# Hash-masked attention and a two-layer block on one core: score products in bursts of three key tiles, one hash for q and k, another order

## The chip, the core and the metric

The kernel runs on one core of a Trainium2 chip. The core has five engines that work side by side, each through its own queue in order: TensorE (PE, matrix products; its weight loads are shown as PEld), VectorE (DVE), ScalarE (ACT), GpSimd (POOL) and SyncE (SP, which here only issues DMAs). An engine waits for another one by semaphores. Matrix products are written to PSUM, which has eight banks of 512 fp32 values on each of 128 partitions; all else lies in SBUF. The metric is the device time of one execution in microseconds (us); lower is better.

## The reference, cut to what matters

```python
# q, k, v: 4 batches, 8 heads, 768 rows, 64 columns; proj: 64 x 6
q_bits = (einsum('bhsd,dk->bhsk', q, proj) > 0)      # six bits for each row
k_bits = (einsum('bhsd,dk->bhsk', k, proj) > 0)
mask   = q_bucket[:, :, :, None] == k_bucket[:, :, None, :]
scores = where(mask, (q @ k.T) / 8, -1e9)
attn   = exp(scores - max);  attn = attn / (sum(attn) + 1e-9)
x      = (attn @ v) with the heads side by side      # 4 x 768 x 512
xn     = (x - mean) / sqrt(var + 1e-6) * g_ln
out    = x + relu(xn @ w_ch1) @ w_ch2                # 512 -> 2048 -> 512
```

A query attends only to the keys with the same six bits.

## The kernel before, in words

The rows are cut into 12 units of 256 query rows, three to each batch of 768 rows. Within a unit the eight heads form two groups of four.

**Scores.** A step `S.s` is one unit, one head group and one pair of key tiles (128 keys each), so there are 72 steps. For each key tile and each of the four heads three products accumulate: one over the hash bits (line 569, tile `G`; 6 rows, 32 in the first batch) and two over the halves of the 64 columns (32 rows each, tiles `qb`, `kb`). The four heads sit in four groups of 32 rows of TensorE, each writing its own bank, so that four products run beside each other. Equal bits give a term so large that the exponential of all others vanishes. A step fills two tiles of two banks each (`sc`, tag `pp`, three such slots, six banks). ACT takes the exponential of each with `E.s.h` (line 575) into `E`, and `A.s` (line 594) multiplies it with the values and a column of ones into `acc`, which takes one of the same three slots. The other two banks (tag `f`) serve everything else on TensorE.

**From attention to output.** On DVE `na` and `nb` divide by the row sums, `nc` and `ag` take mean and variance, `ce` normalises into `xc`; `fl` transposes it by DMA into `xnT` (in unit 0 TensorE does this with `ft`, and `fc` on DVE scales by `g_ln`). `F.u.p` (line 658) is a piece of the first layer, 256 of the 2048 hidden columns: it reads columns 256 p to 256 p + 255 of `w1_sb`. `R` applies the relu on ACT or DVE. The second layer is `D` and `Z` in unit 0; the later units use seven half-sized products `P` with sums `ss` and `Y` (lines 725 and 730). `O` writes the output.

**Hash.** For batch 0 the row-wise q and k are transposed in 128 x 256 pieces (`tn`), hashed (`ha`, `hc`, `sl`, lines 393, 404, 417) and cast (`ca`). For later batches `LX` loads one head group of q or k (786 KB) with SP, `tu` transposes it on DVE into `T` (two slots, one tile for q and one for k), `CA` casts it, and `hm` (line 525) hashes it, 16 fp32 products of 192 columns, q's and k's apart. `bt` takes the signs, `mw` and `mr` spread the bits through DRAM into `G`.

**Weights.** `lw1.n` and `lw2.n` load a quarter of each weight matrix, with a cast from fp32 to bf16, from POOL's queue (lines 445 and 456): `lw1.n` brings columns 512 n to 512 n + 511 of `w1_sb`, `lw2.n` the rows 512 n to 512 n + 511 of the second matrix. `wg` later multiplies `g_ln` into `w1_sb`, `sw` makes the sums of weights that `P` uses.

**Order.** Nothing plans at run time. The string `ORDER` lists every operation as name, engine letter (t TensorE, v DVE, a ACT, p POOL, s SP) and indices; each engine's queue has its own words in that order. `SLOTS` gives, for each tag, the slot that each tile takes in turn. Semaphores between engines follow from the tiles that operations share. A DMA waits in its issuing engine's queue, and all behind it wait too.

Of the kernel before, what the change touches and what calls it, by code (L numbers as in the profile page):

```python
# [10 lines left out]
AOP = mybir.AluOpType  # L11
# [5 lines left out]
lp.a lx.a.0.1.0.1 lx.s.0.0.0.1 lx.s.0.1.1.3 lx.s.1.1.0.3 lx.s.1.0.0.1 lv.s.0.0.4 lx.s.0.0.1.3 lv.s.0.4.4 lx.s.1.0.1.3  # L17
lg.s on.p.0 mem.v tab.a pf.v warm.t wm.t.0 wm.t.1 sel.p tn.v.0.0.0
p32.p tn.v.0.1.0 on.p.1 ca.a.0.0.0 pmem.p ha.t.0.0.0 bh.v.0.0.0 ha.t.0.1.0 bh.v.0.1.0 wm.t.2
wm.t.3 ca.a.0.1.0 tn.v.0.1.1 ca.p.0.1.1 tn.v.0.1.2 S.t.0.2 E.a.0.0 E.a.0.1 ha.t.0.1.1 bh.v.0.1.1  # L20
ha.t.0.1.2 bh.v.0.1.2 wm.t.6 tn.v.1.1.1 ca.p.1.1.1 lw1.p.3 ca.a.0.1.2 tn.v.1.1.0 S.t.1.2 E.a.1.1
tn.v.1.0.0 ha.t.1.1.1 bh.v.1.1.1 cv.p.0.0.0 tn.v.1.1.2 gx.p.1.0.0 S.t.2.2 cv.p.0.0.2 cv.p.0.4.2 ca.p.1.1.2
E.a.1.0 ca.a.1.0.0 lv.s.1.0.3 lw1.p.1 ha.t.1.0.0 bh.v.1.0.0 gx.p.1.0.1 LX.s.1.0.0 ha.t.1.1.2 bh.v.1.1.2
E.a.2.1 lw1.p.0 ca.v.1.1.0 LX.s.1.0.1 tn.v.0.0.1 S.t.4.2 E.a.2.0 lv.s.1.0.2 ca.v.0.0.1 E.a.4.1
ha.t.1.1.0 A.t.0.2 A.t.2.2 sq.t.0.0 E.a.4.0 bh.v.1.1.0 S.t.3.2 sc.v.0.0 A.t.1.2 cv.a.0.4.0
E.a.3.1 hc.t.0.0.1 E.a.3.0 lw2.p.0 na.v.0.0 S.t.5.2 bc.v.0.0.1 sl.t.0.0.1 bi.v.0.0.1 E.a.5.1
sq.t.0.4 tn.v.1.0.1 S.t.8.2 hc.t.1.0.1 nb.v.0.0 nc.v.0.0 E.a.5.0 bc.v.1.0.1 E.a.8.0 A.t.4.2
A.t.5.2 sc.v.0.4 A.t.3.2 na.v.0.1 nb.v.0.1 E.a.8.1 sl.t.1.0.1 ca.a.1.0.1 bi.a.1.0.1 S.t.6.2
gt.t E.a.6.0 nc.v.0.1 ag.v.0.1 S.t.7.2 ag.v.0.0 ce.v.0.1 ft.t.0.1 ce.v.0.0 gc.v
E.a.6.1 E.a.7.0 ft.t.0.0 S.t.9.2 E.a.7.1 E.a.9.0 fc.v.0.1 E.a.9.1 fc.v.0.0 F.t.0.3  # L30
A.t.7.2 R.a.0.3 F.t.0.7 R.a.0.7 S.t.10.2 tn.v.1.0.2 E.a.10.0 tu.v.1.0.1.2 gx.p.1.1.0 LX.s.1.1.0
lw1.p.2 tu.v.1.0.1.3 tu.v.1.0.0.3 lv.s.1.0.1 E.a.10.1 tn.v.0.0.2 hc.t.0.0.2 ca.a.0.0.2 tu.v.1.0.1.0 A.t.6.2
bc.v.0.0.2 sl.t.0.0.2 F.t.0.6 R.a.0.6 lw2.p.3 A.t.8.2 bi.v.0.0.2 S.t.11.2 F.t.0.0 tu.v.1.0.0.1
hc.t.1.0.2 tu.v.1.0.1.1 gx.p.1.1.1 LX.s.1.1.1 na.v.1.0 tu.v.1.0.0.0 lw2.p.1 E.a.11.0 rs.p.0 tu.v.1.0.0.2
R.v.0.0 E.a.11.1 CA.v.1.0.0 S.t.14.2 E.a.14.0 nb.v.1.0 bc.v.1.0.2 E.a.14.1 hm.t.1.0 ca.v.1.0.2
lv.s.1.0.0 S.t.12.2 wg.v.3 sl.t.1.0.2 bi.a.1.0.2 bt.v.1.0 mw.s.1.0 mr.s.1.0.1 A.t.11.2 A.t.10.2
tu.v.1.1.0.3 E.a.12.1 A.t.9.2 CA.p.1.0.1 na.v.1.1 nb.v.1.1 mr.s.1.0.2 mr.s.1.0.0 tu.v.1.1.0.1 tu.v.1.1.0.2
E.a.12.0 nc.v.1.0 F.t.0.2 R.a.0.2 S.t.13.2 E.a.13.1 su.p.1.0 F.t.0.4 F.t.0.5 R.v.0.5
S.t.16.2 lw2.p.2 E.a.13.0 A.t.12.2 E.a.16.0 A.t.13.2 A.t.14.2 tu.v.1.1.0.0 F.t.0.1 E.a.16.1
tu.v.1.1.1.1 tu.v.1.1.1.3 R.a.0.4 na.v.2.0 tu.v.1.1.1.2 tu.v.1.1.1.0 nc.v.1.1 nb.v.2.0 R.a.0.1 S.t.15.2  # L40
E.a.15.0 nc.v.2.0 mr.s.1.0.3 ag.v.1.0 E.a.15.1 hm.t.1.1 S.t.17.2 D.t.0.0.0 sw.v.3.1 E.a.17.0
ag.v.1.1 rs.p.1 bt.v.1.1 D.t.0.0.1 wg.v.1 lv.s.1.4.3 A.t.16.2 A.t.15.2 E.a.17.1 A.t.17.2
na.v.2.1 nb.v.2.1 mw.s.1.1 S.t.18.2 ce.v.1.1 LX.s.2.0.0 mr.s.1.1.3 fl.s.1.1 mr.s.1.1.1 nc.v.2.1
sw.v.2.1 ce.v.1.0 fl.s.1.0 cv.p.1.0.0 wg.v.2 wg.a.0 D.t.0.1.0 ag.v.2.0 sw.v.4.1 ag.v.2.1
mr.s.1.1.0 E.a.18.1 mr.s.1.1.2 D.t.0.1.1 sw.v.1.1 D.t.0.0.2 cv.a.1.0.2 CA.a.1.1.0 S.t.20.2 E.a.20.1
lv.s.1.4.2 E.a.20.0 D.t.0.0.3 Z.v.0.0 D.t.0.1.2 D.t.0.1.3 Z.v.0.1 S.t.19.2 F.t.1.6 E.a.18.0
rs.p.2 F.t.1.3 CA.p.1.1.1 E.a.19.0 S.t.21.2 O.s.0.0 lv.s.1.4.1 E.a.19.1 A.t.19.2 E.a.21.0
R.v.1.6 sw.v.3.0 sw.v.2.0 E.a.21.1 F.t.1.0 R.a.1.0 lv.s.2.0.3 R.v.1.3 ce.v.2.1 sw.v.4.0
lv.s.1.4.0 ce.v.2.0 F.t.1.5 A.t.20.2 S.t.22.2 fl.s.2.1 tu.v.2.0.0.2 F.t.1.4 R.a.1.5 cv.p.1.4.0
A.t.18.2 E.a.22.0 R.v.1.4 F.t.1.2 sp.t.1.0 sc.v.1.0 na.v.3.0 E.a.22.1 S.t.23.2 F.t.1.7  # L50
R.a.1.2 R.v.1.7 E.a.23.1 cv.v.1.4.2 E.a.23.0 F.t.1.1 sw.v.1.0 fl.s.2.0 LX.s.2.0.1 R.a.1.1
nb.v.3.0 S.t.24.2 E.a.24.0 E.a.24.1 on.p.2 P.t.1.2 Y.v.1.2 F.t.2.1 R.a.2.1 su.p.1.4
# [36 lines left out]
nc.v.6.1 F.t.5.5 tu.v.3.1.1.1 ag.v.6.0 S.t.48.2 E.a.48.0 ag.v.6.1 E.a.48.1 tu.v.3.1.1.2 tu.v.3.1.0.2
F.t.5.1 R.v.5.1 A.t.46.2 rs.p.6 R.a.5.5 ce.v.6.1 fl.s.6.1 A.t.45.2 A.t.47.2 na.v.7.1  # L90
# [698 lines left out]
```

## Time and profile before

| | before |
|---|---|
| three runs | 291.16, 291.59 and 295.0 us, median 291.59 |
| profiled execution, first to last instruction (span) | 289.9 us; the page gives no other time for it |
| PE busy | 283.2 us (98%) |
| DVE, ACT, POOL busy | 207.5, 206.2, 53.5 us |
| exponentials on ACT (line 575) | 144, 153.1 us |
| first-layer products (line 658) | 768, 94.2 us |
| score products (line 569) | 1728 |
| granted TensorE clock | 0.997 |
| DMA moved | 34.10 MB |

A row of a group of instructions gives line, engine, operation, output and inputs, shapes and count; then busy time and the mean length of one in ns; then the idle time of the engine before them and what ended it. Busy time of PE contains the modelled ends of pipelined products, which overlap. The page's slices cut the span into 40 parts of 7.2 us; a digit of 9 is 90% or more. In a table by windows the columns are the stretch, its length, busy time and count of PE, PEld, DVE, ACT and POOL, the granted clock, the share of the 16 DMA engines that was busy (it may pass 1.00, since packets overlap) and GB/s. Queue q1 is that of the DMAs that SP issues, q0 that of POOL's loads. The row of a DMA issue ends with the time from issue to landing, where the trace has it.

### The profile page before, as it was taken

What the parts mean: (1) busy time and instruction counts of PE and PEld (TensorE: products, weight loads), DVE (VectorE), ACT (ScalarE), POOL (GpSimd) and SP (SyncE); (2) the same over time, 40 slices, a digit from 0 to 9 for tenths busy, and PEclk for the clock granted to TensorE, in tenths of its full rate; (3) what the DMA queues carried; (4) which work ended last, traced back from release to release, by engine and by line L of the source; (5) the groups of instructions that cost most, each with busy time, mean ns of one, the idle gap of its engine ahead of it and who ended that gap; (6) DMA issues with size and microseconds to landing.
All of it is one profiled execution on the core that took longest, in us unless ns stands there. A gap on an engine that the chain in (4) does not pass through costs nothing.

```text
span 289.9 us, 10600 instructions
## 1 busy us (share of the span) xinstructions
PE 283.2 (98%) x4685; PEld 228.1 (79%) x4687; DVE 207.5 (72%) x478; ACT 206.2 (71%) x236; POOL 53.5 (18%) x88
## 2 busy tenths in 40 slices
PE   8999999999999999999999999999999999999994
PEld 4777777658788887888778778877888888898883
DVE  5758899987878895787568985866665645782653
ACT  4889999998866978775865897887794694515140
POOL 4560426232241005001200108210010010001000
PEclk9999999999999999999999999999999999999998
DMA  6999997646634791385430352230321301404022
GB/s 224 363 291 269 207 277 125 164 106 162 199 104 130 142 353 28 124 109 154 79 86 3 84 133 63 57 66 2 93 21 20 75 0 29 102 2 101 10 72 74
DMA packets 31055, 34.10 MB, mean 118 GB/s; under 512 B 15521, under 2 KB 27809, under 8 KB 31010
## 3 DMA queue, kind: packets, MB, share of 16 engines
q1 hardware_dynamic: 25938, 28.72, 36.6%
q0 software_dynamic: 4224, 4.19, 8.8%
q8 instruction: 36, 0.59, 0.9%
q10 hardware_dynamic: 848, 0.53, 0.7%
q14 instruction: 9, 0.07, 0.1%
HBM read 27.86 MB, written 6.88 MB: 120 GB/s over the span
## 4 chain that ended last, share of the span: by engine, by line
PE 95%; DVE 2%; ACT 1%; issue 0%; ACTq 0%; DVEq 0%
PE f L658 30%; PE sc L569 18%; PE X L725 13%; PE acc L594 12%; PE Yb L725 7%; PE Ya L725 3%; PE hp L525 3%; PE hf L393 3%; PE f L673 2%; PE warm L363 1%; ACT E L575 1%; DVE xnT L651 0%; PE warm L367 0%; PE hf L404 0%; PE vp L486 0%; PE Yc L725 0%
## 5 line engine op out<-in xcount | busy, mean ns | idle before, releaser
L575 ACT ACTIVATE E<-sc,bias_sb 128x1024 bf16<-128x1024 f32 x144 | 153.1, 1111 | 33.7 <-PE sc L569 30.4
L658 PE MATMUL f<-xnT,w_sb 128*128 128x256 bf16 x768 | 94.2, 273 | 0.1
L658 PEld LDWEIGHTS <-w_sb 128*128 128x128 bf16 x768 | 71.5, 98 | 12.6 <-issue 4.8
L666 ACT ACTIVATE hb<-f 128x512 bf16<-128x512 f32 x67 | 39.6, 598 | 33.7 <-PE f L658 33.7
L569 PE MATMUL sc<-qb,kb 32*128 32x256 bf16 x1152 | 52.5, 268 | 0.0
L594 PEld LDWEIGHTS <-E 128*128 128x128 bf16 x1152 | 40.8, 98 | 3.8 <-issue 2.5
L594 PE MATMUL acc<-vaug,E 128*128 128x65 bf16 x1152 | 43.5, 194 | 0.0
L569 PE MATMUL sc<-G 6*128 6x256 bf16 (+1 forms) x576 | 42.7, 273 | 0.8 <-ACT E L575 0.8
L725 PEld LDWEIGHTS <-hb 128*128 128x128 bf16 x352 | 33.3, 98 | 5.4 <-issue 1.3
L569 PEld LDWEIGHTS <-kb 32*128 32x128 bf16 x1152 | 30.6, 93 | 1.5
L634 POOL TENSOR_SCALAR rs<-mv 128x2 f32<-128x2 f32 x12 | 3.3, 277 | 151.3 <-DVE mv L623 151.2
L730 DVE TENSOR_TENSOR x<-X,x 128x256 f32<-128x256 f32 x44 | 18.4, 419 | 15.6 <-PE X L725 15.3
L725 PEld LDWEIGHTS <-S 128*128 128x128 bf16 x264 | 24.9, 98 | 4.5 <-issue 1.3
L569 PEld LDWEIGHTS <-G 6*128 6x128 bf16 (+1 forms) x576 | 16.1, 91 | 15.6 <-issue 13.1
L668 DVE TENSOR_SCALAR hb<-f 128x512 bf16<-128x512 f32 x29 | 19.7, 680 | 12.0 <-PE f L658 11.8
L304 DVE STREAM_TRANSPOSE T<-X 128x384 f32<-128x384 f32 (+2 forms) x52 | 26.1, 534 | 0.0
L725 PE MATMUL Yb<-w_sb,S 128*128 128x256 bf16 x176 | 22.9, 273 | 0.0
L607 DVE SCALAR_TENSOR_TENSOR y<-vsB,acc 128x520 f32<-128x520 f32 x24 | 16.5, 689 | 7.8 <-PE acc L594 7.6
L725 PE MATMUL X<-wt,hb 128*128 128x256 bf16 x168 | 21.8, 273 | 0.0
L616 DVE TENSOR_TENSOR x<-y,rc 128x512 f32<-128x512 f32 x24 | 17.9, 747 | 0.8
L620 DVE BATCH_NORM_STATS2 st<-x 128x6 f32<-128x256 f32 x48 | 17.4, 411 | 0.2
L730 DVE TENSOR_TENSOR x<-Yb,x 128x256 f32<-128x256 f32 x22 | 9.2, 420 | 9.7 <-PE Yb L725 9.6
(95 smaller groups left out, 267.4 us busy)
## 6 DMA issues: line engine op xcount, KB each, us to landing
out_dram<-x SPq DMA_DIRECT2D x45, 128.0 KB
X<-in_k_dram SPq DMA_DIRECT2D x7, 768.0 KB
vn<-in_v_dram SPq DMA_DIRECT2D x24, 192.0 KB
X<-in_q_dram SPq DMA_DIRECT2D x6, 768.0 KB
w_sb<-in_moe_w_ch_dram POOLq DMA_DIRECT2D x8, 512.0 KB, 11.5
vn<-in_v_dram SPq DMA_DIRECT2D x2, 768.0 KB
X<-in_q_dram SPq DMA_DIRECT2D x2, 512.0 KB
Bd<-B SPq DMA_DIRECT2D x6, 96.0 KB
```

What stands on the lines that cost most here:

```text
L304: nc.vector.transpose(d[:, j], s[:, j, kj0 : kj0 + n])
L569: nc.tensor.matmul(sc(s, i // 2)[:, i % 2, 256 * kk : 256 * kk + 256], lh, rh, start=(rep == 0), stop=(rep == 2), skip_group_check=True,)
L575: nc.scalar.activation(E(s)[:, heads(h)], sc(s, h), AF.Exp, scale=EXP_SCALE, bias=bias_sb)
L594: nc.tensor.matmul(acc[:, qt, (D + 1) * i : (D + 1) * (i + 1)], E(s)[:, i, 256 * kk + P * qt : 256 * kk + P * qt + P], vaug(u // 3)[:, 4 * ...
L607: nc.vector.scalar_tensor_tensor(yt(u, g), vs, EPS_ROW, made[f"acc{u}{g}"][:, :, :A], op0=AOP.mult, op1=AOP.add,)
L616: nc.vector.tensor_tensor(xo, a[:, :, :, 0:D], rc.to_broadcast([P, 2, 4, D]), op=AOP.mult)
L620: nc.vector.bn_stats(stats(u)[:, qt, g], xt(u)[:, qt, 256 * g : 256 * g + 256])
L658: nc.tensor.matmul(f1[:, n].rearrange("p (t x) -> p t x", t=2), w1_sb[:, dt, P * nt : P * nt + P], xnT(u)[:, :, dt], start=(dt == 0), stop ...
L666: nc.scalar.activation(hb(u)[:, 2 * p : 2 * p + 2], f1, AF.Relu)
L668: eng.tensor_scalar_max(hb(u)[:, 2 * p : 2 * p + 2], f1, 0.0)
L725: nc.tensor.matmul(f2, lh[:, n], rh[:, n], start=(first and n == 0), stop=(n == 7), skip_group_check=True)
L730: nc.vector.tensor_tensor(x, made[f"{prod(u, k)}{u}"], x, op=AOP.add)
```

## The change

Units 0 to 2 keep pairs of key tiles; in units 3 to 11 the scores of three key tiles at once use all six banks of tag `pp`. A word `S.t.u.g.k` is now one key tile of one head group (12 products), so 144 words replace 72. `spots` says which bank each key tile and head takes. In a burst of three, the lower heads (0, 1) of its first tile and the upper heads (2, 3) of its third share a pair of banks, one in each half. Two row groups may then write to one bank, and a new operation keeps them apart: `N`, an empty instruction on ACT, waits for the first tile's last product of the lower heads and raises a semaphore, for which the third tile's first product of the upper heads waits. Each burst still makes three pairs of banks and three exponentials of 128 x 1024, so there are 144 exponentials as before; `A` works on one such pair (8 products).

`hm` hashes q and k with the same products: 8 of 384 columns; `T` is one tile for both, with one slot. The tiles `tp`, `xc`, the sums `S` of the second layer and the partial sums of v (now `t2`, one step smaller) take slots of 2 KB among the 14 that the exponentials `E` use; `E` had four slots of 4 KB.

`ORDER` is written anew throughout. POOL's queue at the start has the casts, weight loads and small memsets in another order; so has SP's, where the load of k of batch 0 is the first on ACT's queue ahead of `proj`, and loads of batch 2 (`LX.2.0.0`, `LX.2.0.1`) stand much earlier. The warming products `warm` and `wm` are the same in number.

```diff
 ORDER = """
 # POOL's words, first part
-on.p.0 sel.p p32.p on.p.1 pmem.p ca.p.0.1.1 ca.p.1.1.1 lw1.p.3 cv.p.0.0.0 gx.p.1.0.0 cv.p.0.0.2 cv.p.0.4.2 ca.p.1.1.2 lw1.p.1 gx.p.1.0.1 lw1.p.0 lw2.p.0 gx.p.1.1.0 lw1.p.2 lw2.p.3 gx.p.1.1.1 lw2.p.1 rs.p.0 CA.p.1.0.1 su.p.1.0 lw2.p.2
+ca.p.0.1.1 on.p.0 gx.p.1.0.1 sel.p ca.p.1.1.1 cv.p.0.0.2 cv.p.0.0.0 p32.p gx.p.1.0.0 lw1.p.3 on.p.1 ca.p.1.1.2 lw2.p.1 gx.p.1.1.1 lw1.p.0 lw1.p.2 lw2.p.2 gx.p.1.1.0 cv.p.0.4.2 lw2.p.3 lw2.p.0 pmem.p CA.p.1.0.1 lw1.p.1 rs.p.0
 # SP's words after the loads of batch 0
-lv.s.1.0.3 LX.s.1.0.0 LX.s.1.0.1 lv.s.1.0.2 LX.s.1.1.0 lv.s.1.0.1 LX.s.1.1.1 lv.s.1.0.0 mw.s.1.0
+LX.s.1.0.1 LX.s.1.0.0 LX.s.1.1.1 lv.s.1.4.1 lv.s.1.0.0 lv.s.1.4.2 lv.s.1.4.0 LX.s.2.0.0 LX.s.1.1.0 LX.s.2.0.1 lv.s.1.0.3 mw.s.1.0
 # TensorE's words up to the first pieces of the first layer
-S.t.0.2 ha ha S.t.1.2 ha S.t.2.2 ha ha S.t.4.2 ha A.t.0.2 A.t.2.2 sq S.t.3.2 A.t.1.2 hc S.t.5.2 sl sq S.t.8.2 hc A.t.4.2 A.t.5.2 A.t.3.2 sl S.t.6.2 gt S.t.7.2 ft ft S.t.9.2 F.t.0.3 A.t.7.2 F.t.0.7 S.t.10.2
+S.t.0.0.1 S.t.0.0.0 ... S.t.1.1.1 S.t.1.1.0 hm.t.1.0 S.t.1.1.2 S.t.1.1.3 sl.t.0.0.2 A.t.1.0.0.0 A.t.1.0.1.0 ft.t.0.1 A.t.1.0.1.1 ft.t.0.0 A.t.1.0.2.0 A.t.1.0.0.1 A.t.1.0.2.1 S.t.1.1.4 S.t.1.1.5 F.t.0.0 F.t.0.2 A.t.1.1.0.1
 # a burst of unit 8
+S.t.8.1.0 N.a.8.1.0 S.t.8.1.1 E.a.8.1.0.1 O.s.4.0 mw.s.3.1 S.t.8.1.2 E.a.8.1.0.0 E.a.8.1.0.2
...
+TYPES = "222222333333333333333333"
...
 def hm(eng, b, g):
-        for t in range(2):
-            for j in range(2):
-                for c in range(4):
-                    nc.tensor.matmul(
-                        hp[32 * c : 32 * c + 32, W * t : W * t + W], p32[:, j], Tt(b, g, t)[:, j, W * c : W * c + W],
-                        start=(t == 0 and j == 0), stop=(j == 1), skip_group_check=True,
-                    )
+        for j in range(2):
+            for c in range(4):
+                nc.tensor.matmul(
+                    hp[32 * c : 32 * c + 32, : 2 * W].rearrange("p (t w) -> p t w", t=2), p32[:, j],
+                    Tt(b, g)[:, :, j, W * c : W * c + W], start=(j == 0), stop=(j == 1), skip_group_check=True,
+                )
...
+    def spots(u, g):
+        if TYPES[2 * u + g] == "2":
+            return {(k, i): (k // 2, i // 2, i % 2, k % 2) for k in range(KJ) for i in range(4)}
+        at = {}
+        for k in range(KJ):
+            for i in range(4):
+                lower, n = i < 2, k % 3
+                pair, half = {0: ((0, 0), (1, 0)), 1: ((2, 0), (1, 1)), 2: ((2, 1), (0, 1))}[n][0 if lower else 1]
+                at[k, i] = (k // 3, pair, i % 2, half)
+        return at
...
+    def S_(eng, u, g, k):
+        b, q0, k0, at = u // 3, 256 * (u % 3), P * k, spots(u, g)
+        for rep in range(3):
+            for i in range(4):
...
+                a, p, bank, half = at[k, i]
+                m = nc.tensor.matmul(
+                    sc(u, g, a, p)[:, bank, 256 * half : 256 * half + 256], lh, rh,
+                    start=(rep == 0), stop=(rep == 2), skip_group_check=True,
+                )
+                if TYPES[2 * u + g] == "3":
+                    if k % 3 == 0 and rep == 2 and i == 1:
+                        ended[u, g, a] = m.ins.name
+                    if k % 3 == 2 and rep == 0 and i == 2:
+                        m.wait_op(shared, passed[u, g, a], "sem-ge")
+
+    def N_(eng, u, g, a):
+        m = eng.nop()
+        tc.add_manual_dep(m.ins, ended[u, g, a], after, reason="the bank goes on to another row group")
+        m.then_inc(shared, 1)
+        passed[u, g, a] = len(passed) + 1
```

More of the change, by code (lines that the diff above doesn't have):

```diff
@@ L16 @@
 ORDER = """
[L17 to L28, printed above, removed]
```

358 lines of the change are left out of this document (180 added, 178 removed).

## The prediction

> **What bounds the kernel now.** I read the page first: busy time per engine, the span in 40 slices, the queues and the chain that ended last.
>
> ```profile
> PE 283.2 (98%) x4685; PEld 228.1 (79%) x4687; DVE 207.5 (72%) x478; ACT 206.2 (71%) x236; POOL 53.5 (18%) x88
> PE   8999999999999999999999999999999999999994
> ...
> DMA  6999997646634791385430352230321301404022
> ...
> q0 software_dynamic: 4224, 4.19, 8.8%
> ...
> PE 95%; DVE 2%; ACT 1%; issue 0%; ACTq 0%; DVEq 0%
> PE f L658 30%; PE sc L569 18%; PE X L725 13%; PE acc L594 12%; PE Yb L725 7%; PE Ya L725 3%; PE hp L525 3%; PE hf L393 3%; PE f L673 2%; PE warm L363 1%; ACT E L575 1%; DVE xnT L651 0%; PE warm L367 0%; PE hf L404 0%; PE vp L486 0%; PE Yc L725 0%
> ```
>
> TensorE is the bound and the chain runs on it; the other engines have a quarter of the span to spare. So only two things move the end: TensorE work that goes, and time in which it stands still. The DMA row is low on the whole, but its first slices are full. TensorE's timeline, the chain from 19 to 32 us and the DMA queues by window show both places more closely:
>
> ```profile
> 29.62 1.30 DVE xnT L651 x2
> 30.96 1.03 PE f L658 x8
> ```
> ```profile
> DMA  9999999999999999928999999999999951059995
> ...
> q0 software_dynamic: 4224, 4.19, 65.5%
> q1 hardware_dynamic: 2031, 4.63, 35.2%
> ```
>
> The second fence is the stretch from 15 to 54 us. The first-layer product (L658) begins at 30.96, held by DVE's normalisation, and after that TensorE always has work. Yet through those 39 us the DMA engines are nearly always full: the eight weight loads on POOL's queue (q0) take 65.5% of them and everything of SP's queue (q1) 35.2%. The weights got there in time because each chunk of columns was asked for long before its product. That cover is what I watch.
>
> **Part 1: score blocks, a gain.** Between products of 128 rows and score products of 32 or 6 rows TensorE loses time at both ends:
>
> ```profile
> 149.80 0.60 PE L725 MATMUL Ya<-w_sb,hb 128*128 128x256 bf16 x4
> 150.33 0.29 PE L569 MATMUL sc<-G 6*128 6x256 bf16 x4
> 150.45 0.39 PE L569 MATMUL sc<-qb,kb 32*128 32x256 bf16 x8
> 150.67 0.28 PE L569 MATMUL sc<-G 6*128 6x256 bf16 x4
> 150.78 0.39 PE L569 MATMUL sc<-qb,kb 32*128 32x256 bf16 x8
> 151.10 1.05 PE L725 MATMUL X<-w_sb,hb 128*128 128x256 bf16 x8
> 151.99 1.04 PE L725 MATMUL Yb<-w_sb,S 128*128 128x256 bf16 x8
> 152.86 1.04 PE L725 MATMUL X<-wt,S 128*128 128x256 bf16 x8
> ```
>
> Eight full products take 151.99 to 152.86, 0.109 each. Four take 0.44 of the 0.53 before the block: 0.09 lost going in. Inside, three sets of four score products take 0.34 (150.33 to 150.67), so six take 0.68 of the block's 0.77: 0.09 lost coming out. A block thus costs 0.18 beside its products. TensorE's order, counted in both programs, has 72 blocks before and 62 after: not 54, because nine key tiles stand alone and units 0 to 2 keep pairs. Ten blocks at 0.18 are **1.8 us**. The number of score products, exponentials (144) and value products is unchanged.
>
> **Part 2: the hash, near nothing.** `hm` takes 8 products of 384 columns for 16 of 192.
>
> ```profile
> L525 PE MATMUL hp<-T,p 128*32 128x192 f32 x192 | 9.2, 330 | 0.0
> L393 PE MATMUL hf<-tp,pfull 128*128 128x256 f32 x32 | 8.3, 398 | 0.0
> L404 PE MATMUL hf<-tp,p 128*32 128x64 f32 x64 | 1.7, 225 | 0.0
> ...
> L417 PE MATMUL hf<-Bc,spread 128*128 128x64 bf16 x16 | 1.1, 194 | 0.0
> ```
>
> Four of the first run beside each other, so a group of 192 columns takes 9.2/48 = 0.19 us, 1.0 ns a column; the second form, 256 columns, takes 0.26, also 1.0 ns. Cost goes by columns, and those stay. The third form (64 columns, 0.106 a group) would leave some 0.06 fixed per group, 1.5 us in all for 24 groups fewer. I take **0.2**, by the row nearest in shape; bounds 0 and 1.5. (The last row is `sl`, for part 4.) The price is that q and k now share one tile with one buffer: the next head group's transposes wait for this one's hash and both casts. They are on DVE, 72% busy; zero, and up to 1.4 us (one hash) five times if that cover fails.
>
> **Part 3: the new wait, small.** In a burst of three key tiles a bank goes to another row group for the third tile. An empty instruction on ACT (36 in all) waits for the first tile's last lower-head product, and TensorE waits for it. Behind it on ACT stand this burst's exponentials; behind TensorE's wait, everything.
>
> ```profile
> 151.22 1.11 ACT L575 ACTIVATE E<-sc,bias_sb 128x1024 bf16<-128x1024 f32 x1 [2.27 <-PE sc L569]
> ```
> ```profile
> 21.87 1.12 ACT E L575
> 22.99 0.04 issue
> 23.04 0.83 PE sc L569 x22
> ```
>
> A score product's end (150.78 + 0.39) reaches ACT in 0.05, and ACT's end (22.99) reaches TensorE in 0.05. The product in question starts two sets into the burst (0.23) and lasts 0.27; with both legs, 0.60. The third tile is due at six sets, 0.68. Back to back (24 cases by the order) it just fits if ACT is free; elsewhere other products lie between. If an exponential stands in front it costs up to 1.11, over 36 bursts 40 us. But the exponentials in front are those whose banks the burst itself needs. Where only three full-product blocks separate two bursts (2.6 us) the three exponentials (3.2 us) end about where the second tile needs the third bank pair. The trace has no such wait; bounds 0 and 40, and I take **+1.0**, near the lower end since the order leaves ACT its turn.
>
> **Part 4: the head, where I expect the loss.** POOL's load order changes from w1 chunks 3, 1, 0, w2 0, w1 2, w2 3, 1, 2 to w1 3, w2 1, w1 0, w1 2, w2 2, 3, 0 and last w1 1. But the second product of the first layer, `F.0.2`, reads columns 512 to 767, chunk 1: the eighth load. Its weight load waits for it, and TensorE's whole queue stands behind that, ACT's `R.0.2` too.
>
> When would TensorE be there? In front of `F.0.2` stand, beyond what stood before 30.96: two score calls (0.77 each), three value calls (12% of the chain over 72, 0.48 each), a hash (9.2/6), two each of `hc` and `sl` (a quarter of 1.7 and of 1.1 each, 1.4 together) and `F.0.0` (30% over 96, 0.9). That is 6.8, so 37.8. Arriving then, the run ends as before less parts 1 and 2; each later microsecond is lost, since TensorE has no idle time to repay it from.
>
> When would chunk 1 be there?
>
> ```profile
> q1 hardware_dynamic: 3535, 4.15, 81.0%
> ```
> ```profile
> 12.45 1.00 POOL L445 DMA_DIRECT2D w_sb<-in_moe_w_ch_dram  x1
> ...
> 18.36 0.75 POOL L445 DMA_DIRECT2D w_sb<-in_moe_w_ch_dram  x1
> ```
> ```profile
> X<-in_k_dram SPq DMA_DIRECT2D x7, 768.0 KB
> ...
> vn<-in_v_dram SPq DMA_DIRECT2D x24, 192.0 KB
> ```
> ```profile
> 15.00:21.00 6.00, 5.67 (x130) 4.35 (x132) 3.65 (x9) 5.20 (x7) 4.39 (x7) 1.00 1.15 288
> ...
> 42.00:45.00 3.00, 3.00 (x77) 2.49 (x74) 2.77 (x6) 2.82 (x4) 1.02 (x1) 1.00 1.25 211
> ```
>
> The first row is the window up to 15 us: 4.15 MB of the first batch's 4.72 (four X of 0.786, two v as large) are in. That stays, for SP issues the same loads. From 15 us until chunk 1 lands the engines must move all eight weight loads: 65.5% of 39 us, 25.5. From q1, at 35.2% of 39 us for 4.63 MB, 2.97 a megabyte, they move at least the remaining 0.57 MB, three X of batch 1 and four v pieces (3.7 MB, 11.0). At most come the fourth X, two X of batch 2 that SP now issues ahead of it or right behind, and a v piece (6.3 MB, 18.6). The sum is 36.5 to 44.1; in full stretches the summed share reads 1.15 (extreme 1.25), so 31.7 to 38.4 us: landing at 46.7 to 53.4, at 44.2 if all goes at 1.25. I take **50.0**, the middle. SP's move counts too: `LX.1.1.0` stands behind the X load of batch 2, which waits for DVE, and DVE's transpose of it stands ahead of the scaling that `F.0.0` needs. The stall hides this, though alone it could cost some 3 us.
>
> So the stall is 50.0 - 37.8 = **12.2 us**. While it lasts, ACT and DVE get ahead, which repays nothing.
>
> The Trainium skill's page "DMA: Bandwidth & Descriptors", section "Anatomy of one DMA — SWDGE (gpsimd) path", fits one such DMA as 2.0 us plus its bytes at 436 GB/s: an estimate of 4.4 us for 1 MiB read. By it `F.0.2` would hardly wait, and the sum would be the first rival's. The trace disagrees where loads queue:
>
> ```profile
> w_sb<-in_moe_w_ch_dram POOLq DMA_DIRECT2D x1, 512.0 KB, 8.6
> ```
> ```profile
> w_sb<-in_moe_w_ch_dram POOLq DMA_DIRECT2D x1, 512.0 KB, 15.0
> ```
> ```profile
> w_sb<-in_moe_w_ch_dram POOLq DMA_DIRECT2D x1, 512.0 KB, 5.7
> ```
>
> These are the loads issued at 12.45, at 33.72 behind two others, and at 47.67 alone. The same page, section "Queues, rings and completion order", has each DMA engine take turns between queues, which would fit q0's and q1's equal parts.
>
> **The rest at zero.** Small tiles in the exponentials' slots, three smaller adds on POOL (18% busy), a second table touch on ACT: other engines' slack covers them. The projection is now issued behind k; its copies ended a microsecond before the first transpose, which q's arrival released, so a little later is free:
>
> ```profile
> 2.40 0.74 DVE L351 COPY pfull<-prj 32x12 f32<-32x12 f32 x4 [0.57 <-DMA prj<-in_proj_dram]
> ...
> 4.08 1.65 DVE L304 STREAM_TRANSPOSE tp<-X 128x256 f32<-128x256 f32 x4 [0.94 <-DMA X<-in_q_dram]
> ```
>
> Sum: 289.9 - 1.8 - 0.2 + 1.0 + 12.2 = 301.1 of span; the median of the three runs, 291.6, is 1.7 above the profiled span, so **302.8 us**.
>
> **Rivals.**
> 1. *Chunk 1 lands in time.* Were SP's loads passed by and the eight weight loads alone on the engines from 17 us on, 25.5 at 1.25 is 20.4, and the last lands near 37.4. Decisive point: landing at 37.8. Then 289.9 - 2.0 + 1.0 + 1.7 = 290.6, not slower. For it: POOL is 18% busy and could issue early. Against it: its queue holds casts that wait for DVE and for v, and the engines are full.
> 2. *The ACT wait takes over.* An exponential stands in front of half the 36 waits: 18 x 1.11 = 20 on top of the sum without part 3, 322; with the weights in time 310. For it: ACT is in order and 71% busy. Against it: the banks already force that order.
> 3. *The bursts do not form.* If alternating fillers break them, part 1 goes: 1.8 more, 304.6, inside my range.
>
> **How the numbers follow.** Forecast (a weight stall of 6 to 16 us) 0.77, first rival 0.12, second 0.06, other mishaps 0.05. From a landing at 44.2 without part 3 (296.0) and some room below for a part of the q1 work passed by, to 53.4 with part 3 at 3 us (308.2) and a little above: 294.5 to 309, which leaves out the two rivals, 0.18. A measurement of this kernel can tell about 2% from no change, 285.8 to 297.4 here: slower 0.81 (forecast mostly, second rival, half the mishaps), same 0.17, faster 0.02.
>
> **What would show it.** In the profile after: a TensorE gap of some 12 us near 38 us, released by a DMA of `w_sb` at the line of `F`; full DMA slices up to 50; ten score blocks fewer; hash groups of 0.38; few gaps at score products. I am wrong if the eighth load lands by 40, or if many short gaps follow the empty instructions.

## The result, and the profile after

The changed kernel takes **320.29 us** (median of 4 runs, 318.19 to 322.42), the kernel before 291.48 beside it: a ratio of **1.0967** (95% interval 1.0891 to 1.1044). The forecast was 302.8, in a range of 294.5 to 309. The sign was right and the size was not. Times and ratios leave out executions more than 1.5% above the fastest of their kernel; the traces of two runs below, the second mended version and the kernel before with the projection second, are of such executions.

The page of the changed kernel (busy time, the span of 318.3 us in 40 slices, the chain, and the weight loads with their median from issue to landing):

```profile
PE 288.5 (91%) x4588; PEld 228.3 (72%) x4591; DVE 214.8 (67%) x478; ACT 205.7 (65%) x236; POOL 55.0 (17%) x88
...
PE   6997940599699999999999999999999999999994
...
PEclk9998895599999999999999999999999999999999
DMA  7959999211418829243126012103030210412322
...
PE 78%; DMA 12%; DVE 5%; issue 1%; POOL 1%; SPq 0%; ACTq 0%; ACT 0%; DVEq 0%; POOLq 0%
PE f L680 26%; PE sc L589 15%; PE X L747 12%; PE acc L617 9%; DMA w_sb<-in_moe_w_ch_dram 9%; PE Yb L747 6%; PE hf L402 3%; PE Ya L747 3%; PE hp L533 2%; DVE w_sb L462 1%; DMA xnT<-xc 1%; DMA prj<-in_proj_dram 1%; PE f L695 1%; DVE S L732 1%
...
w_sb<-in_moe_w_ch_dram POOLq DMA_DIRECT2D x8, 512.0 KB, 25.9
```

TensorE had 98% and now has 91% of a longer span. The hole is in slices 6 to 8, and in slices 7 and 8 the granted clock is at half. The chain, 95% TensorE before, now runs 12% over DMAs, 9% of it (29.6 us) over one weight load. What TensorE's products waited for, summed by releaser (us in total, times, longest):

```profile
PE f L680 <- DMA w_sb<-in_moe_w_ch_dram: 13.8, 1, 13.8
PE sc L589 <- DVE y L629: 3.2, 2, 2.8
PE f L680 <- DVE xnT L673: 2.1, 1, 2.1
PE hf L402 <- DVE tp L313: 1.8, 1, 1.8
PE sc L589 <- ACT E L606: 1.7, 2, 1.2
```

The first row is the forecast stall at `F.0.2`, 13.8 us where 12.2 was forecast. The others stood in no term of the sum. The 2.1 us for `xnT`, in front of `F.0.0`, are what the prediction named beside its sum: VectorE waited for `LX.1.1.0`, whose transpose stands ahead of the scaling.

```profile
42.38 0.58 DVE L313 STREAM_TRANSPOSE T<-X 128x384 f32<-128x384 f32 x1 [2.54 <-DMA X<-in_q_dram]
```

The stall hides them here, as the prediction said, since chunk 1 landed far later. Three places explain the rest.

**The head.** TensorE's and VectorE's timelines of the changed kernel, the chain in its first microseconds, and TensorE's timeline of the kernel before:

```profile
6.52 3.52 PE L402 MATMUL hf<-tp,pfull 128*128 128x256 f32 x8 [1.81 <-DVE tp L313]
...
10.56 0.29 PE L589 MATMUL sc<-G 32*128 32x256 bf16 x4
```
```profile
5.29 0.70 DVE L360 COPY pfull<-prj 32x12 f32<-32x12 f32 x4 [3.47 <-DMA prj<-in_proj_dram]
```
```profile
1.51 3.76 DMA prj<-in_proj_dram
```
```profile
4.87 2.07 PE L393 MATMUL hf<-tp,pfull 128*128 128x256 f32 x8
...
7.45 0.29 PE L569 MATMUL sc<-G 32*128 32x256 bf16 x4
```

The projection, issued behind k's load, lands after 3.76 us. VectorE's copies wait 3.47 for it, TensorE stands 1.81, and its eight hash products then take 3.52 instead of 2.07. The first score product comes 3.1 us later, and all that hangs on it: POOL's casts, and behind them its weight loads.

**The weight loads and the clock.** Windows of the changed kernel (window, its length, busy time and count of PE, PEld, DVE, ACT and POOL, granted clock, DMA share, GB/s), and the DMA queues from 15 to 59 us:

```profile
15.00:20.00 5.00, 5.00 (x63) 3.53 (x62) 4.07 (x12) 4.63 (x6) 4.23 (x9) 1.00 0.46 183
20.00:25.00 5.00, 5.00 (x141) 4.02 (x143) 4.17 (x13) 4.63 (x6) 5.00 (x11) 1.00 0.87 220
45.00:50.00 5.00, 0.31 (x3) 0.03 (x1) 4.37 (x10) 0.00 (x0) 0.83 (x1) 0.72 1.22 225
50.00:55.00 5.00, 0.00 (x0) 0.00 (x0) 0.00 (x0) 0.00 (x0) 0.00 (x0) 0.50 1.22 222
55.00:60.00 5.00, 0.94 (x5) 0.70 (x6) 0.00 (x0) 0.00 (x0) 0.00 (x0) 0.50 0.58 96
60.00:65.00 5.00, 5.00 (x63) 3.74 (x62) 0.00 (x0) 1.87 (x3) 0.00 (x0) 0.58 0.00 0
```
```profile
q0 software_dynamic: 4224, 4.19, 58.6%
q1 hardware_dynamic: 2180, 6.33, 40.1%
```

From 15 to 25 us the engines are not full (0.46 and 0.87): the first weight load is issued at 19.6 instead of 12.45. The eight loads then take 58.6% of 44 us, 25.8, and SP's queue 40.1%, 17.6 for 6.33 MB. The last load is issued at 29.4 and lands at 59.0. The clock falls to 0.50 while TensorE waits and is at 0.58 in the five microseconds after.

**POOL beside VectorE.** VectorE's and POOL's timelines of the changed kernel, ahead of the 2.8 us wait in the second row of waits:

```profile
76.27 4.33 DVE L462 TENSOR_SCALAR w_sb<-w_sb,gT 128x512 bf16<-128x512 bf16 x4
```
```profile
76.02 1.46 POOL L488 TENSOR_TENSOR t<-vn 128x512 f32<-128x512 f32 x1
77.56 1.26 POOL L489 TENSOR_TENSOR t<-t,vn 128x512 f32<-128x512 f32 x1
78.90 0.73 POOL L490 TENSOR_TENSOR vsum<-t 128x256 bf16<-128x256 f32 x1
79.57 0.89 POOL L483 CAST vaug<-vn 128x768 bf16<-128x768 f32 x1
```

VectorE's four scalings of a w1 chunk take 4.33 us. Four instructions of POOL run in the same time and sum to 4.34. In the kernel before, where no adds of POOL stand beside them, four scalings take 1.13:

```profile
54.81 1.13 DVE L453 TENSOR_SCALAR w_sb<-w_sb,gT 128x512 bf16<-128x512 bf16 x4
```

**Where the 28.4 us of span lie.** I counted every product at its usual pitch (a full one 0.109, a value product 0.029, four score products 0.1135, a score block 0.19 beside them) and took the sum from what TensorE really needed. The table gives the time beyond that count. TensorE's last product ends 28.4 later; what follows it takes 4.2 us in both.

| stretch of TensorE's order | before, us | after, us |
|---|---|---|
| start to the first first-layer product | 4.1 | 12.1 |
| `F.0.0` to `F.0.2` (the weight stall) | - | 13.9 |
| `F.0.2` to `F.0.3` (the lowered clock) | - | 2.4 |
| from there to `F.1.6` (POOL beside VectorE) | 0.3 | 3.0 |
| `F.1.6` to the end (units 1 to 11) | 2.2 | 4.9 |
| the count itself | 279.1 | 277.7 |

### The profile page after: what moved, and what is told of

The parts are those of the page before. It is cut to its first block, busy times and chain, and to the rows that moved or that the text cites. A ratio compares the mean times of both kernels' runs of the same rounds, so it can differ in the third digit from the quotient of the medians.

```text
span 318.3 us, 10475 instructions
## 1 busy us (share of the span) xinstructions
PE 288.5 (91%) x4588; PEld 228.3 (72%) x4591; DVE 214.8 (67%) x478; ACT 205.7 (65%) x236; POOL 55.0 (17%) x88
## 4 chain that ended last, share of the span: by engine, by line
PE 78%; DMA 12%; DVE 5%; issue 1%; POOL 1%; SPq 0%; ACTq 0%; ACT 0%; DVEq 0%; POOLq 0%
PE f L680 26%; PE sc L589 15%; PE X L747 12%; PE acc L617 9%; DMA w_sb<-in_moe_w_ch_dram 9%; PE Yb L747 6%; PE hf L402 3%; PE Ya L747 3%; PE hp L533 2%; DVE w_sb L462 1%; DMA xnT<-xc 1%; DMA prj<-in_proj_dram 1%; PE f L695 1%; DVE S L732 1%; DVE T L313 1%
## 5 line engine op out<-in xcount | busy, mean ns | idle before, releaser
L680 PE MATMUL f<-xnT,w_sb 128*128 128x256 bf16 x768 | 95.3, 275 | 16.6 <-DMA w_sb<-in_moe_w_ch_dram 13.8
L589 PE MATMUL sc<-G 6*128 6x256 bf16 (+1 forms) x576 | 42.0, 274 | 5.0 <-DVE y L629 3.2
L617 PEld LDWEIGHTS <-E 128*128 128x128 bf16 x1152 | 42.1, 99 | 3.2 <-issue 0.8
L617 PE MATMUL acc<-vaug,E 128*128 128x65 bf16 x1152 | 44.4, 196 | 0.0
L656 POOL TENSOR_SCALAR rs<-mv 128x2 f32<-128x2 f32 x12 | 2.6, 218 | 193.4 <-DVE mv L645 193.4
L589 PEld LDWEIGHTS <-G 6*128 6x128 bf16 (+1 forms) x576 | 16.8, 91 | 19.7 <-issue 17.1
L638 DVE TENSOR_TENSOR x<-y,rc 128x512 f32<-128x512 f32 x24 | 16.7, 697 | 5.0 <-issue 2.7
L651 DVE TENSOR_SCALAR xc<-x,mv,rs 128x512 bf16<-128x512 f32 x22 | 13.5, 625 | 3.1 <-POOL rs L657 3.0
## 6 DMA issues: line engine op xcount, KB each, us to landing
w_sb<-in_moe_w_ch_dram POOLq DMA_DIRECT2D x8, 512.0 KB, 25.9
```

The source lines that it names most:

```text
L589: m = nc.tensor.matmul(sc(u, g, a, p)[:, bank, 256 * half : 256 * half + 256], lh, rh, start=(rep == 0), stop=(rep == 2), skip_group_check ...
L617: nc.tensor.matmul(acc[:, qt, (D + 1) * i : (D + 1) * (i + 1)], Ep(u, g, a, p)[:, bank, 256 * half + P * qt : 256 * half + P * qt + P], va ...
L638: nc.vector.tensor_tensor(xo, a[:, :, :, 0:D], rc.to_broadcast([P, 2, 4, D]), op=AOP.mult)
L680: nc.tensor.matmul(f1[:, n].rearrange("p (t x) -> p t x", t=2), w1_sb[:, dt, P * nt : P * nt + P], xnT(u)[:, :, dt], start=(dt == 0), stop ...
```

## The experiments

All times are compared with the kernel before on the same chip (291.4 to 292.1). The four runs of the changed kernel spread over 4.2 us, so a difference of 3 or 4 us between two medians counts here only where the traces show it at the place meant.

### The projection first

```diff
-lx.a.0.1.0.1 lp.a mem.v
+lp.a lx.a.0.1.0.1 mem.v
```

> The changed kernel with one edit: the projection's load is issued ahead of k's again. Theory (a late projection shifts the whole head): in the changed kernel the projection landed 3.76 us after its issue, TensorE stood from 4.7 to 6.5 us, its clock was halved and the first score product began at 10.55 instead of 7.45. With the edit that product begins near 7.5, the first weight load is issued some 3 us earlier, and as the DMA engines move the same bytes from there on, chunk 1 lands near 56 instead of 59: 320.3 - 3 = 317 us (315 to 318). Rival (chunk 1's landing is set by bytes on full DMA engines alone, from the start): the head gains 3 us, the wait at F.0.2 grows by 3, and the time stays at 320.

Measured: 317.2 us (ratio 1.0883, 1.0832 to 1.0935). The first score product comes at 8.06, the eighth load is issued at 26.9 and lands at 56.0. The theory holds: against the changed kernel the first score product and the eighth load's issue come 2.5 us earlier, and the landing 3.0. The late projection moves the whole head, and through POOL's queue the landing. Its price is not a fixed one: the eight hash products behind a late projection take between 1.99 and 3.78 us in the seven runs that have it.

### Chunk 1 second

```diff
-sq.t.0.0 S.t.0.1.1 lw1.p.3 bh.v.1.1.2
+sq.t.0.0 S.t.0.1.1 lw1.p.3 lw1.p.1 bh.v.1.1.2
...
-lw1.p.1 LX.s.1.1.0
+LX.s.1.1.0
```

> The changed kernel with one edit: the load of w1 chunk 1 is issued second of the eight instead of last. Theory (the order of the loads is the cause): chunk 1 lands near 35, before TensorE comes to F.0.2 at about 45; the wait of 13.9 us goes and with it about 2.1 us at a lowered clock behind it: 320.3 - 16 = 304 us (301 to 307). Rival (the wait only passes on, to the next chunk, to w2 or to ACT, whose waits the stall covered): 312 us or more, with a new wait of over 5 us behind F.0.2.

> The changed kernel with both edits, projection first and chunk 1 second. Theory: the two add, 304 - 3 = 301 us (298 to 304), that is still some 10 us above the kernel before, which would then be in places other than the weight stall and the head (a stall of 3 us at the value-row sums, and many small waits). Rival (the changed kernel's loss is the two edits alone): 290 to 293, the time of the kernel before.

Measured: 312.9 (1.0740, 1.0700 to 1.0779), and with the projection first 310.6 (1.0657, 1.0620 to 1.0694). The first theory was 9 us too fast; the rival's time came true, though its new wait stands ahead of `F.0.2` and not behind it. Of the pair with both edits neither forecast came true. TensorE's waits with chunk 1 second:

```profile
PE f L680 <- DMA w_sb<-in_moe_w_ch_dram: 6.0, 1, 6.0
PE sc L589 <- DVE y L629: 4.4, 2, 4.0
...
PE f L680 <- DVE B L316: 1.5, 1, 1.5
```

The wait passed on. `F.0.0` now waits 6.0 us for chunk 0, which had become the fourth load and landed at 46.7. And w2 chunk 0, now the eighth, landed at 58.0 and held VectorE's sums for the seven-product form, so that `F` waited 1.5 for a bank behind them (`B`). "One chunk is in the wrong place" was too simple: a load that moves forward moves the others back.

### The stall filled with products

```diff
         f1 = ps(f"f1_{u}{p}", [P, 2, 256], "f")
+        if (u, p) == (0, 2):
+            for _ in range(124):
+                nc.tensor.matmul(f1[:, 0].rearrange("p (t x) -> p t x", t=2), ones, xnT(u)[:, :, 0], start=True, stop=True)
```

> The changed kernel with 124 needless products of 128x256 (0.109 us each, 13.5 us in all) in front of F.0.2, where TensorE would wait for chunk 1; they write to F.0.2's bank, which F.0.2 then begins anew. Theory (standing still lowers the granted clock, and getting it back costs about 2 us): chunk 1 lands near 59 as before, the granted clock from 50 to 60 is 1.0 instead of 0.50, F.0.2's eight products take 1.05 instead of 1.89, and the time is 320.3 - 2.1 = 318.2 us. Rival (the slow products behind the stall come from elsewhere, or ACT and DVE gained nothing during it): 320 or more, with F.0.2 still at 1.9.

Measured: 319.6 (1.0961, 1.0927 to 1.0995). Its windows and TensorE's timeline:

```profile
50.00:55.00 5.00, 5.00 (x49) 4.49 (x46) 0.20 (x1) 0.00 (x0) 0.58 (x1) 1.00 1.22 221
55.00:60.00 5.00, 4.68 (x44) 3.97 (x42) 0.00 (x0) 0.00 (x0) 0.00 (x0) 1.00 0.74 124
60.00:65.00 5.00, 5.00 (x96) 4.40 (x96) 0.00 (x0) 3.05 (x4) 0.00 (x0) 1.00 0.02 3
80.00:85.00 5.00, 3.80 (x39) 1.99 (x39) 4.93 (x11) 2.91 (x4) 2.65 (x3) 0.71 0.51 138
```
```profile
59.95 1.05 PE L685 MATMUL f<-xnT,w_sb 128*128 128x256 bf16 x8 [0.32 <-DMA w_sb<-in_moe_w_ch_dram]
```
```profile
81.20 0.29 PE L589 MATMUL sc<-G 32*128 32x256 bf16 x4 [2.79 <-DVE y L629]
```

The clock stays at 1.00 and `F.0.2` takes 1.05 us instead of 1.89. From `F.0.2` to the score product behind the next wait it is 21.25 us (59.95 to 81.20) instead of 23.60 (59.06 to 82.66): 2.35 saved, as the theory had it. The sum does not show it, for two reasons. Chunk 1 landed 0.9 later here. And the 2.8 us wait at 81.2, which left the clock at 1.00 in the changed kernel, brought it to 0.71 here; from that product to the last one it takes 232.8 instead of 231.1, and 1.6 of these 1.7 us are lost by 85.3.

### The value-row sums left out

POOL's six adds for batch 1 become two memsets; the second batch's output lacks their part.

```diff
     def su(eng, b, hs):
+        if b == 1:
+            taken["E"] = taken.get("E", 0) + 1
+            nc.gpsimd.memset(vsum(b)[:, D * hs : D * (hs + 4)], 0.0)
+            return
```

> The changed kernel without the value-row sums of batch 1: POOL's six adds are replaced by two memsets of zero, so the second batch's output lacks the part that the sums carry. Theory (POOL's adds slow VectorE's bf16 work to a third, and TensorE's stall of 3.15 us at 82.66 comes from that): VectorE's four scalings of w1 chunk 2 take 0.35 us each instead of 1.08, its two normalisations near them 0.5 to 0.6 instead of 1.5, TensorE's stall there goes, and the time is 320.3 - 3 = 317 us (316 to 318.5). Rival (VectorE is slow there for another reason, or it is late and not slow): the scalings stay at about 1.08 and the time at 320.

Measured: 316.3 (1.0813, 1.0736 to 1.0889), 4.0 less than the changed kernel. The traces put it lower: from `F.0.3` to `F.1.6` TensorE needs 21.95 us (65.66 to 87.61) instead of 24.79 (64.78 to 89.57), 2.8 less. VectorE's timeline:

```profile
74.32 1.08 DVE L462 TENSOR_SCALAR w_sb<-w_sb,gT 128x512 bf16<-128x512 bf16 x4
...
77.40 1.81 DVE L462 TENSOR_SCALAR w_sb<-w_sb,gT 128x512 bf16<-128x512 bf16 x4
```

The second four take 1.81 instead of 4.33, and TensorE's wait is gone. Casts of POOL are still beside them and beside the first of the two normalisations, which takes 1.92 and not the 0.5 to 0.6 expected. This is the Trainium skill's page "SBUF — State Buffer", section "SBUF: two separate sides": a VectorE instruction in a two-port mode, or with two inputs in SBUF, shares one port pair with GpSimd, and whoever starts first holds it for the whole instruction. The trace agrees in the time: four scalings last as long as four instructions of POOL, 4.33 and 4.34; it does not show the mode.

### Batch 2's X loads later

```diff
-lw2.p.0 pmem.p CA.p.1.0.1 LX.s.2.0.0 bc.v.0.0.2
+lw2.p.0 pmem.p CA.p.1.0.1 bc.v.0.0.2
...
-ce.v.0.1 LX.s.2.0.1 sl.t.0.0.2
+ce.v.0.1 sl.t.0.0.2
...
-lv.s.1.4.3 fc.v.0.1
+lv.s.1.4.3 LX.s.2.0.0 LX.s.2.0.1 fc.v.0.1
```

> The changed kernel with batch 2's two X loads (1.57 MB) issued on SP behind the last value load that stands ahead of F.0.0, instead of ahead of and right behind batch 1's last X load. Theory (chunk 1's landing is set by the bytes that the DMA engines move till then; in the changed kernel 6.33 MB of SP's queue took 17.6 us from 15 to 59 us, 2.78 a megabyte): chunk 1 lands 4.4 us earlier, at 54.6, and the time is 320.3 - 4.4 = 315.9 us. Rival (POOL's queue of weight loads runs at a pace of its own): chunk 1 lands at 59 and the time stays at 320.

Measured: 319.6 (1.0945, 1.0842 to 1.1047), no change. But the trace shows that the step did not do what I meant: the two loads were issued at 37.7 and 38.2, and chunk 1 landed at 58.0, 30.0 us after its issue (29.6 in the changed kernel), so they were still moved before it. The same two loads further back:

```diff
-lv.s.1.0.2 mr.s.1.0.0
+lv.s.1.0.2 LX.s.2.0.0 LX.s.2.0.1 mr.s.1.0.0
```

> The changed kernel with batch 2's two X loads issued on SP behind the value load that stands behind F.0.1, so that they start after chunk 1 has landed (moved less far, they were issued at 37.7 and were still moved before it). Theory (chunk 1's landing is set by all bytes that the DMA engines move till then; where the mended version issued these loads at 50.5, its eighth weight load landed at 50.9 instead of 55.0): chunk 1 lands 4 us earlier, at 54 to 55.5, and the time is 320.3 - 4 = 316.3 us (315 to 318). Rival (POOL's queue has a pace of its own): chunk 1 lands at 58 to 59 and the time is 319 to 321.

Measured: 316.3 (1.0841, 1.0810 to 1.0872), as forecast. The eighth weight load, from issue to landing, in the changed kernel (issued at 29.4) and here (29.2):

```profile
w_sb<-in_moe_w_ch_dram POOLq DMA_DIRECT2D x1, 512.0 KB, 29.6
```
```profile
w_sb<-in_moe_w_ch_dram POOLq DMA_DIRECT2D x1, 512.0 KB, 26.5
```

1.57 MB fewer ahead of it save 3.1 us of flight, `F.0.2` begins 3.3 us earlier (55.76), and the time is 4.0 less; by the queue's own rate (17.6 us for 6.33 MB) it would be 4.4. So SP's loads do delay POOL's weights.

### The loads in the order of need, and three mended versions

The first puts the projection first and changes what stands in the eight places of POOL's order:

```diff
-lw1.p.3 ... lw2.p.1 ... lw1.p.0 lw1.p.2 lw2.p.2 ... lw2.p.3 ... lw2.p.0 ... lw1.p.1
+lw1.p.0 ... lw1.p.1 ... lw1.p.3 lw1.p.2 lw2.p.0 ... lw2.p.2 ... lw2.p.1 ... lw2.p.3
```

> The changed kernel with the projection first and the eight weight loads in the order in which they are needed: w1 chunks 0, 1, 3, 2, then w2 0, 2, 1, 3. Theory (what put chunk 1 second left open is again the order of the loads: there chunk 0, as the fourth load, landed at 46.7 and w2 chunk 0, as the eighth, held VectorE's sums for the seven-product form): no wait on a weight load over 1 us is left before 60 us, the time is 310.6 - 5.2 (wait at F.0.0) - 0.8 (wait for VectorE) - 1 (clock) = 303.5 us (301 to 306). Rival (whatever the order, 8 MiB of weights can't be there in time, and the wait passes on to the fourth or sixth load): 309 to 311.

Measured: 305.2 (1.0436, 1.0352 to 1.0519), within the theory's bounds. TensorE waits for no weight load any more. VectorE does, 2.7 us at the sums of w2, where the theory allowed none over 1 us, and TensorE's wait for `y`, behind scalings that stand beside POOL's adds, is still there with 4.0 us.

The mended version adds to it (words of one engine each: SP, POOL, POOL, VectorE; the scratch tile of the sums takes another slot for it):

```diff
-LX.s.2.0.0 LX.s.1.1.0 LX.s.2.0.1 ... lv.s.1.0.2
+LX.s.1.1.0 ... lv.s.1.0.2 LX.s.2.0.0 LX.s.2.0.1
...
-cv.p.1.4.0 rs.p.1 CA.p.1.1.1 su.p.1.0 cv.p.1.0.0 su.p.1.4 rs.p.2
+cv.p.1.4.0 su.p.1.4 rs.p.1 CA.p.1.1.1 cv.p.1.0.0 rs.p.2 su.p.1.0
...
-sw.v.3.0 ... sw.v.2.0 ... na.v.2.0
+sw.v.3.0 sw.v.2.0 na.v.2.0
```

> The changed kernel with everything found so far put right at once: projection first, weight loads in the order of need, batch 2's X loads later, the value-row sums of batch 1 away from VectorE's scalings, and VectorE's sums of w2 (lines of sw.3.0 and sw.2.0) behind its scalings. Theory (the loss is made up of head, weight stall, clock and the sums' contention, and the bursts themselves are worth at most 2 us): 320.3 - 3 - 14 - 2.5 - 3 - 1 = 297 us, still above the kernel before by its small waits (294 to 300). Rival (the bursts' own waits cost nothing and the rest was all in the named places): 289 to 291, faster than before by the ten blocks. Second rival (another wait takes the stall's place): 303 or more.

Measured: 299.3 (1.0238, 1.0160 to 1.0316), within the theory's bounds. Its eighth load takes 24.6 us to land instead of 28.6, again the price of the two X loads. What is left of the larger waits: 2.4 us for a transposing DMA that took 7.3 us behind an X load, and 1.0 us at an exponential near 25, around which the granted clock is 0.70 (24 to 27 us) and then 0.50 (27 to 30).

The second mended version:

```diff
-CA.p.1.1.1 cv.p.1.0.0 rs.p.2 su.p.1.0
+CA.p.1.1.1 cv.p.1.0.0 su.p.1.0 rs.p.2
...
-LX.s.3.0.1 ... fl.s.2.1
+fl.s.2.1 LX.s.3.0.1
...
-gt.t S.t.1.0.4 S.t.1.0.5 S.t.1.0.0
+S.t.1.0.4 S.t.1.0.5 gt.t S.t.1.0.0
```

> The mended version with three more moves: the four products that turn the gain vector stand between two score pairs (so that they cover a wait for an exponential), batch 3's X load is issued behind the transposing DMA of unit 2 (which took 7.3 us behind it), and POOL's remaining sums of batch 1 stand ahead of unit 2's normalisation. Theory (what is left over the kernel before is head waits with a lowered clock, 2.4 us for the transposing DMA and 1.6 us at VectorE's normalisation): 299.3 - 1.5 - 2.4 - 1.5 = 294 us (292 to 297). Rival (the waits are replaced by others, since VectorE is full between 50 and 80 us): 298 to 300.

Measured: 297.9 (1.0219, 1.0178 to 1.0259), between the theory's bounds and the rival's. I had put POOL's sums back beside VectorE's scalings, which took 4.33 us again in the trace, and TensorE waited 3.2 us for `y` at 63.3.

The third, against the mended version:

```diff
-su.p.1.4 rs.p.1 CA.p.1.1.1 cv.p.1.0.0 rs.p.2 su.p.1.0
+su.p.1.4 su.p.1.0 rs.p.1 CA.p.1.1.1 cv.p.1.0.0 rs.p.2
...
-LX.s.3.0.1 ... fl.s.2.1
+fl.s.2.1 LX.s.3.0.1
...
-lv.s.1.0.3 ... lv.s.1.0.1 mw.s.1.1 lv.s.1.0.2 LX.s.2.0.0 LX.s.2.0.1
+lv.s.1.0.3 lv.s.1.0.1 lv.s.1.0.2 ... mw.s.1.1 LX.s.2.0.0 LX.s.2.0.1
```

> The mended version with batch 1's value-row sums on POOL all ahead of unit 1's reciprocal root, where VectorE has no scalings and no sums of w2 (two value loads are issued earlier for it), and with batch 3's X load behind unit 2's transposing DMA. Theory (in the second mended version the sums had come back beside VectorE's scalings and cost TensorE 3.2 us; away from them, and without the 2.4 us of the transposing DMA, nothing of that size is left): 299.3 - 2.4 - 1 = 296 us (294 to 297.5), still above the kernel before. Rival (VectorE's work between 50 and 80 us is late whatever stands beside it): 298 to 300.

Measured: 298.0 (1.0210, 1.0192 to 1.0228), 0.5 above the theory's bounds. Its VectorE timeline holds the contention twice, with and without POOL's adds (45.7 to 52.6 us) beside the scalings:

```profile
46.90 3.71 DVE L463 TENSOR_SCALAR w_sb<-w_sb,gT 128x512 bf16<-128x512 bf16 x4
54.19 1.09 DVE L463 TENSOR_SCALAR w_sb<-w_sb,gT 128x512 bf16<-128x512 bf16 x4
```

Of the 28.7 us 22 are thus undone, and the version is still 2% slower than the kernel before. By the count above, taken from one trace and tested by no run, 3.9 of its last 6 us are in the head (two waits for exponentials at 25 and 27 with a granted clock of 0.61 and 0.54 from 24 to 32), 1.5 at `y` near 61, and 1.9 in units 1 to 11, against 1.4 fewer in products. No version that beats the kernel before came out of this.

### The projection second in the kernel before

```diff
-lp.a
+lx.a.0.1.0.1 lp.a
...
-lx.a.0.1.0.1
```

> The kernel before with one part of the change alone: the projection's load is issued behind k's on ACT's queue. Theory (a load of 1.5 KB behind a large one lands more than a microsecond later, and the whole head with it): the projection lands 3.8 us after its issue instead of 1.6, TensorE stands before the first hash products and runs them at a lowered clock, and the time is 291.5 + 3 = 294.5 us (293 to 296). Rival (my forecast's: the copies have a microsecond to spare and the shift is free): 291.5.

Measured: 293.0 (1.0048, 1.0031 to 1.0065). The 1.4 us are real, but half of what was expected. In the trace the projection lands after 3.62 us and the first score product comes at 10.52, 3.1 late; at 30 us TensorE is still 3.4 behind, so this execution gives nothing back. Where the others do isn't shown.

## Why the prediction was right in sign and wrong in size

- **Part 1 (-1.8): right.** 62 blocks, and a longer block costs only its products:

```profile
101.33 1.10 PE sc L589 x36
...
121.13 0.77 PE sc L589 x24
122.88 0.44 PE sc L589 x12
```

  Twelve more cost 0.33, so each block still carries about 0.1 at its end and 0.1 at its start, and ten fewer are 1.8. The count of products fell by 1.4, where parts 1 and 2 together said 2.0, and no run isolates the bursts. The end does not show the gain: units 1 to 11 lose 4.9 us to waits beyond their products, against 2.2 before.
- **Part 2 (-0.2): right.** The hash groups (count, busy us, mean ns), after and before, 9.0 against 9.2:

```profile
L533 PE MATMUL hp<-T,p 128*32 128x384 f32 x96 | 9.0, 492 | 0.0
```

  The single buffer cost nothing: the transposes into `T` waited for a load once (the 2.54 above) and for no hash.
- **Part 3 (+1.0): it measured 0.** Of the 27 bursts of 36 products, 26 last 1.10 to 1.11 us from first to next product; the one that lasts 1.67 waits for VectorE (`y`, 0.38). The rival by ACT's order falls with it.
- **Part 4 (+12.2): the mechanism right, the landing 9 us too early.** The stall measured 13.8, near the forecast by luck: its two ends were wrong by 9.0 and 7.5 us the same way. The *landing* was put at 50.0 (46.7 to 53.4) and came at 59.0. The step that failed is "from 15 us until chunk 1 lands the engines must move" at a share of 1.15. By queue they moved 25.8 + 17.6 = 43.4 us of the 16 engines' time instead of 40.3, the middle, since SP's bytes were at my upper end: 2.7 us. The other 6.3 are the share. It was 0.46 and 0.87 for ten microseconds and the two queues' shares sum to 0.99 over the whole stretch, since I let POOL's loads be there at 15 us and never placed their issue behind the casts ahead of them in POOL's order. The first one was issued 7.1 us later than in the kernel before: the second cast of k began at 15.15 instead of 11.41, and 3.4 us with casts of v and copies now stand between it and the load; no run moves these alone. The *arrival* at `F.0.2` was put at 37.8 and came at 45.3: 3.1 from the projection, 1.7 from two waits for exponentials, 2.1 from the wait for `xnT`, the rest not split further. By itself a late arrival costs nothing as long as chunk 1 lands later still; it counts through the projection alone, which also delayed the loads.
- **"The rest at zero": the step that cost most beside the landing.** The projection "a little later is free" took a copy that ends a microsecond early for cover, but priced the shift at nothing, and the load took 3.76 us instead of some 1.6: 3 us of time by the first experiment, part of the late landing above. "Three smaller adds on POOL (18% busy)" counted POOL's slack and not what they do to VectorE: 2.8 by the traces of the run without them, 4.0 by its median.
- **"The stall repays nothing" was not enough.** It cost 2.35 us more through the granted clock, which no term held.
- **Rivals.** None came. Chunk 1 was far from in time; the sum of the terms without the stall was wrong too, as the run with the loads by need shows: 305.2 and not 290.6.

By terms, against the forecast span of 301.1: landing +9.0, clock +2.4, POOL beside VectorE +2.7 (3.0 against 0.3 before), small waits behind `F.1.6` +2.7 (4.9 against 2.2), part 3 -1.0. That is 15.8 of the 17.2 missing; the other 1.4 are not placed. The small waits are read from one trace and no run tests them.

## What to carry to other kernels

A load that is moved in a queue has two times, its issue and its flight: place the issue first, by the work ahead of it on the issuing engine, and then count every byte that any queue moves before it lands. Mending one late transfer shows little where others stand just behind it: putting chunk 1 second gained 7 of the 16 us expected, and putting all loads in the order of need 5 more. And an engine with 80% of its time free is no free place for work: POOL's adds cost a busy VectorE 3 us.

## What was unexpected of the hardware

- VectorE's bf16 scalings of 128x512, SBUF to SBUF, take 1.09 us for four with little on POOL, 1.69 to 1.81 beside a cast of POOL and 3.71 to 4.33 beside its adds.
- The granted clock changes on a grid. In the changed kernel it falls to 0.50 at 30.12, rises at 33.53, falls at 47.18 and rises at 64.25: 1, 4 and 5 times 3.41 us apart. The changes of the other traces, too, lie whole multiples of 3.41 us apart, with a start of their own in each. The same wait of 2.8 us left the clock at 1.00 in the changed kernel and brought it to 0.50 with the stall filled. Cut at the grid, the first wait (79.89 to 82.66) is shared by two stretches, the second (78.43 to 81.20) lies almost whole in one:

```profile
77.90:81.31 3.41, 1.94 (x15) 0.79 (x9) 3.41 (x4) 2.12 (x2) 3.33 (x4) 1.00 0.16 39
81.31:84.73 3.42, 2.07 (x37) 1.30 (x37) 3.35 (x7) 1.18 (x2) 2.80 (x3) 1.00 0.28 58
```
```profile
78.67:82.09 3.42, 0.89 (x25) 0.67 (x25) 3.35 (x5) 0.15 (x2) 3.26 (x4) 1.00 0.10 23
82.09:85.50 3.41, 3.41 (x16) 1.50 (x15) 3.36 (x8) 3.41 (x5) 0.72 (x1) 0.50 0.80 239
```

  After 1.94 and 2.07 us of TensorE's work in a stretch the next one keeps its clock; after 0.89 it has half. The Trainium skill's page "TensorE: Matmul & The Clock Gate", section "What's actually happening", has the gate judge TensorE by a free-running window of about 3.4 us; these traces agree, with 3.41. Busy time is not the whole rule: in the third mended version a stretch with 2.23 us of work (from 21.46) is followed by 0.50.
- A load of 1.5 KB behind a large one on ACT's queue landed after 3.6 to 3.9 us, against some 1.6 in front of it.
- A 512 KB weight load needs 25.9 us in the median where eight queue up beside 6.3 MB on SP's queue, against 11.5 in the kernel before.
